# A two-part attention kernel: the last segment's memory answers move from the projection stage into the attention's row of turns, and the first turn's scores change banks

## The chip, the cores and the metric

The kernel runs on one core of a Trainium2 chip. The metric is the device time of one execution in microseconds (us); lower is better. A core has TensorE (matmuls; called PE in the profile), VectorE (DVE), ScalarE (ACT), GpSimd (POOL) and SyncE (SP, which here issues most DMA transfers).

## The reference

Two attentions are computed over 2048 tokens of width 576 with 32 heads of 18 columns, and set side by side. A is multi-query attention: all heads share one key and one value head. B splits the tokens into 4 segments of 512 and adds a memory of the earlier segments.

```python
# A
p = softmax(q_h @ k.T * Dh**-0.5);  o_h = p @ v;  out_A = concat(o_h) @ wo
# B, for segments s = 0..3, every head
p = softmax(causal(qs @ ks.T * scale));  a_dot = p @ vs
pq = phi(qs)                           # phi(t) = t + 1 if t > 0 else exp(t)
a_mem = (pq @ M) / (pq @ z + 1e-6)     # M, z from the segments before s
o = g * a_mem + (1 - g) * a_dot        # g = sigmoid(beta), one per head
M, z = M + phi(ks).T @ vs, z + phi(ks).sum(0)
out_B = concat(o) @ wo
```

Asking the memory is thus two products for a segment: `pq @ M` (the numerator) and `pq @ z` (the denominator), for segments 1, 2 and 3.

## The kernel before

The first phase projects the queries, keys and values of A and then of B, segment by segment; a projection (`proj`, L261) is fourteen matmuls of split operands, in tiles of 126 rows (7 heads) and 512 tokens, five tiles for 32 heads. The queries are split into two parts and stored (`split2`, L125 on ScalarE and L127 on VectorE; `store_parts`), `phi` of them is made by ScalarE (L408, L414) and VectorE (L416, `qf`), and `magnitude` writes their absolute values (`aq`, L438), from which `bound` (L588) makes an upper bound of each head's scores in the tile `pu`; `shift_parts` turns it into the shift that is stored for the softmax (`sht`, L136). Where a segment is the last one, `ask` (L444) multiplies each tile's `qf` by the memory, ScalarE evicts it (L451) to `numB[3]`, and `total` (L592) makes the denominators, evicted to `denB[3]` (L627).

The second phase is the attention. Its TensorE, VectorE and ScalarE work is written in the order in which it is issued, as a row of 416 turns. A turn k has three scores (L945 for A, L953 for B; two matmuls each into one of three two-bank buffers called `E`), the exponentials of them (ScalarE, L963; the middle score of a turn is first copied to `W` by VectorE, L960, and then freed; some halves of a tile are done by VectorE as a polynomial, tiles `PD`, L919 to L926), one extra step of TensorE in the bank `F`, and the products with the values (L993, bank `O`) of the scores of turn k - 2. In turns 0 to 18 the extra step is a part of the value sums that the projection stage left over (L513, list `LATER`). From turn 20 (`ASK`) it is a step of the memory for segments 1 and 2 (`ask_memory`, matmuls at L852, two steps for each evicted tile, evictions by VectorE at L857 into `xh` and, for denominators, at L861 into `rb`), once in every turn whose scores are all A's. When memory is through, from turn 64, the extra step is a fill: eight matmuls of the output projection (L796). Blocks of B (one pair of turns) come between blocks of A (eleven turns for a block of four heads): turns 0 to 10 are A's, 11 to 18 B's, 19 to 29 A's, 30 to 37 B's, 38 to 48 A's, 49 to 52 B's, 53 to 63 A's.

All four segments' `qf` and the memories go through DRAM tensors (`qfB[s]`, `mzB`) to the attention, by transfers of SyncE's queue (`load_qf`; the load of `mzB` into the tile `woA` in `ask_memory`).

Of the kernel before, what the change touches and what calls it, by code (L numbers as in the profile page):

```python
# [22 lines left out]
C = 512  # L23
# [36 lines left out]
MZ = 126 + 32  # L60
WB = 1440

LATE_ASK, ASK = (1, 2), 20
LATER = [(2, 14), (3, 14), (0, 3), None, (0, 3), (0, 4), None, (0, 4), None, None, (1, 3), None, (1, 3), None, (1, 2), (1, 2), (1, 2), None, (1, 2)]
FLAG = (2, 9, 11)

# [12 lines left out]
def attention_pair_kernel(ctx, tc, a_xT, a_w, a_wo, b_xT, b_w, b_wo, b_beta, ident_d, hmask_d, bmask_d, cmask_d, sel_d, zmask_d, selx_d, sely_d, out):  # L79
# [82 lines left out]
    with ExitStack() as ph:  # L162
# [248 lines left out]
        def phi(src, R, nm, bufs, hold=lambda ins: ins, e=None):  # L411

            e = e or negative(src, R, hold)
            hold(nc.scalar.activation(e[:R], e[:R], AF.Exp, scale=-1.0))  # L414
            f = p2.tile([128, C], F32, name=nm, bufs=bufs)
            hold(nc.vector.scalar_tensor_tensor(f[:R], src, 0.0, e[:R], op0=ALU.max, op1=ALU.add))  # L416
            return f

        for s in range(NSEG):
# [17 lines left out]
                aqs[t] = p2.tile([128, C], BF, name="aq", bufs=5)  # L437
                hold(nc.scalar.activation(aqs[t][:R], pj[:R], AF.Abs))  # L438

            def ask(t, hold=lambda ins: ins):  # L440
                R = RT[t]
                pn = ps.tile([128, C], F32, name="mm", bufs=1)
                hold(
                    nc.tensor.matmul(  # L444
                        pn[:R], Mst[:R, t].rearrange("p h d -> p (h d)")[:, :R], fs[t][:R], start=True, stop=True
                    )
                )

                def answer():
                    nm = p2.tile([128, C], F32, name="nm", bufs=2)  # L450
                    hold(nc.scalar.activation(nm[:R], pn[:R], AF.Copy, scale=gt[:R, t : t + 1]))  # L451
                    nc.sync.dma_start(numB[s][126 * t : 126 * t + R], nm[:R])

                return answer


            for t in range(5):
                if s == t == 0:
                    pj = ahead
# [25 lines left out]
                if s == 0:  # L485
                    split_wpart(10 + t)
                    if t < 3:
                        load_wpart(12 + t)
            if s and not last:
                nc.sync.dma_start(qfB[s][: RT[4], 4], fs[4][: RT[4]])  # L490
            if s == 0:
                nc.vector.memset(gt, 0.0)
# [94 lines left out]
                R, rows = RT[t], slice(32 * (t % 4), 32 * (t % 4) + 32)  # L587
                hold(nc.tensor.matmul(pu[rows], kbB[:R, t], aqs[t][:R], start=t < 4, stop=t > 0))  # L588

            def total(pd, t):  # L590
                R, rows = RT[t], slice(32 * (t % 4), 32 * (t % 4) + 32)
                pin(nc.tensor.matmul(pd[rows], zst[:R, t], fs[t][:R], start=t < 4, stop=t > 0))  # L592

            for t in range(4) if last else []:
                pj = ps.tile([128, C], F32, name="pj", bufs=4)
                proj(pj[:126], wBh, wBl, xh, xl, 126 * t, 126, pin)
                answer = ask(t - 1 if t else 4, pin)
                if t < 2:
                    (fifth_bound if t else last_key)(pin)
                if t == 3:  # L600
                    pu, pd = (ps.tile([128, C], F32, name="nd", bufs=2) for _ in range(2))
                    for i in (0, 1, 2, 4):
                        total(pd, i)
                e = negative(pj[:126], 126, pin)
                magnitude(t, pj, pin)
                fs[t] = phi(pj[:126], 126, "qf", 5, pin, e)
                answer()
                if t == 3:
                    for i in range(5):
                        bound(pu, i, pin)  # L610
                    answer = ask(3, pin)
                    total(pd, 3)
                    pin(nc.vector.tensor_reduce(fm[:, 1 + s : 2 + s], pu, axis=AX.X, op=ALU.max))
                qp = split2(pt, pj[:126], 126, pin)
                store_parts(qp, 0, 126, qB[s], 7 * t, 7)
                if t == 3:
                    answer()
                    dn = p2.tile([128, C], F32, name="ph_e", bufs=2)
            if not last:
                pu = ps.tile([128, C], F32, name="nd", bufs=2)  # L620
                for t in range(5):
# [2 lines left out]
            sp = shift_parts(pt, pu, -BOUND_UP, C, 128)  # L624
            sent = nc.sync.dma_start(shB[s].rearrange("j r t -> r j t"), sp.bitcast(F32))
            if last:
                nc.vector.tensor_scalar(dn, pd, 1e-6, None, op0=ALU.add)  # L627
                nc.sync.dma_start(denB[s], dn)
# [383 lines left out]

    def by_dve(c, hg):

        return [x for n, x in enumerate(BY_DVE) if n < 2 or (c, hg) in third]

    def turn_of(c, hg):

# [47 lines left out]
    def finish(k, ab, c, hg):  # L1066
# [26 lines left out]

        def place():

            return (ab, c) in parts or len(parts) - filled[0] // FILL < 2 and asked[0] >= min(2, len(parts) + 1)

        def load(k, t):
            load_heads(ab, c, t)
# [31 lines left out]
    with tc.manual_schedule(engines={ENG.PE, ENG.Activation, ENG.DVE}):  # L1131
# [3 lines left out]
        for n, b in enumerate(blocks):  # L1135
            ms = [m for m in range(len(its)) if block_of[m] == n]
            items = [(m, k) for m in ms for k in range(2)]
            for out_, cut in ((turns, len(items) // 3), (prods, len(items) // 3 - 1)):
                ends_ = split(len(items), cut)
                out_ += [items[a:z] for a, z in zip(ends_, ends_[1:])]  # L1140
        at(ASK + 4, 0, lambda: True, lambda k: load_qf(2))

        def halve(hi, lo, src):
            nc.scalar.copy(hi, src)
# [63 lines left out]
        for k in range(len(turns) + 2):  # L1208
            now[0] = k
            exps = [scores(its[n], pr, i == 1) for i, (n, pr) in enumerate(turns[k])] if k < len(turns) else []  # L1210
            for i in (0, 2, 1) if len(exps) == 3 else range(len(exps)):
                exps[i]()
            if k in FLAG:
                loose_flag(k)
            if k < len(LATER) and LATER[k]:
                i, m = LATER[k]
                m0, pj = begun_value.pop(i) if i in begun_value else (0, psO.tile([128, C], F32, name="O" if i == 3 else "F"))
                if m0 + m < 14:
                    begun_value[i] = m0 + m, pj
                late_value(i, m0, m0 + m, pj, (pa.tile([128, D], F32, name="osb", bufs=2) if i > 1 else pa.tile([128, C], F32, name="oe", bufs=4))[:, :304] if m0 + m == 14 else None)  # L1220
            if k > len(turns):
                halve_heads(first, 0)
            if memory is None:
                whole = run_fill()
                while k >= len(turns) and not whole:
                    whole = run_fill()
                if filled[0] % FILL == 0 and k > len(turns):
                    fill.pop(0)
            elif k >= ASK and all(its[n][0] == "A" for n, pr in turns[k]) and next(memory, None) is None:
                memory = None  # L1230

            if k > len(turns):
# [346 lines left out]
```

## Time and profile before

| | |
|---|---|
| median of 3 runs (lowest, highest) | 1394.51 us (1393.42, 1395.25) |
| the profiled execution's own time | 1394.57 us |
| span of its instructions | 1392.9 us |
| busy in the span: TensorE, ScalarE, VectorE, GpSimd | 99%, 87%, 74%, 19% |

The profiled execution is one run, and the time outside its span is 1.7 us. The busy shares are means over stages that have different limits.

### The profile page before, as it was taken

The page shows a single profiled execution, that of the slowest core. Times are in us where ns is not written, and L with a number is a line of the kernel's source. Part 1 is how long each engine was busy: PE and PEld are TensorE (multiplying, and loading weights), DVE is VectorE, ACT ScalarE, POOL GpSimd, SP SyncE. Part 2 cuts the span into 40 slices and gives each one's busy share as a digit, 9 for nine tenths or more (in the row PEclk, how much of TensorE's full clock was granted, in tenths as well). Part 3 has the DMA queues.
Part 4 walks back from the last instruction along what each step waited for, and adds up shares of the span by engine and source line. Part 5 has one row for each costly group of instructions (what it writes and reads, how often), then busy time and mean ns, then how long its engine had stood idle before and what let it go on. Part 6 is the DMA issues. An engine that isn't in the chain of part 4 may idle for free.

```text
span 1392.9 us, 41210 instructions
## 1 busy us (share of the span) xinstructions
PE 1379.1 (99%) x17455; PEld 835.6 (60%) x17455; DVE 1032.6 (74%) x1509; ACT 1205.8 (87%) x1497; POOL 260.5 (19%) x388
## 2 busy tenths in 40 slices
PE   9999999999999999999999999999999999999998
PEld 6778888755554555555555555555555555555558
DVE  6565463388787887777888877876878778887884
ACT  4543453599999999999999999999999999999992
POOL 2462120012313211312110022113010220001002
PEclk9999999999999999999999999999999999999999
DMA  9876556575564545332322442232103321120023
GB/s 285 261 230 185 180 198 204 188 208 181 153 182 158 147 145 162 101 113 77 105 67 71 141 152 63 85 120 79 52 35 100 104 76 42 31 71 21 18 64 132
DMA packets 88638, 173.67 MB, mean 125 GB/s; under 512 B 12308, under 2 KB 20109, under 8 KB 88018
## 3 DMA queue, kind: packets, MB, share of 16 engines
q1 hardware_dynamic: 81614, 158.91, 36.6%
q0 software_dynamic: 2368, 7.13, 1.8%
q10 hardware_dynamic: 4464, 4.92, 1.1%
q8 instruction: 139, 2.28, 0.7%
q14 instruction: 53, 0.43, 0.1%
HBM read 99.65 MB, written 70.67 MB: 122 GB/s over the span
## 4 chain that ended last, share of the span: by engine, by line
PE 88%; DVE 4%; ACT 3%; DMA 2%; issue 1%; POOL 1%; SPq 0%; DVEq 0%; POOLq 0%; ACTq 0%
PE O L993 33%; PE E L945 20%; PE F L796 11%; PE pj L261 11%; PE E L953 3%; ACT P L963 3%; PE nd L513 2%; DVE W L960 2%; PE pj L513 2%; PE E L1280 2%; PE pj L293 1%; PE F L852 1%; PE F L513 1%; DMA wr<-b_w 1%; DMA vseg<-vB 0%
## 5 line engine op out<-in xcount | busy, mean ns | idle before, releaser
L963 ACT ACTIVATE P<-E 128x1024 f32<-128x1024 f32 (+1 forms) x800 | 783.4, 1066 | 2.0 <-PE E L945 1.6
L960 DVE COPY W<-E 128x1024 f32<-128x1024 f32 (+2 forms) x416 | 453.1, 1089 | 142.2 <-PE E L945 84.1
L993 PE MATMUL O<-P,VA 128*32 128x256 f32 x7504 | 506.8, 379 | 0.0
L963 ACT ACTIVATE P<-W 128x1024 f32<-128x1024 f32 (+1 forms) x330 | 366.8, 1112 | 6.8 <-DVE W L960 6.3
L993 PEld LDWEIGHTS O<-P,VA 128*32 128x32 f32 x7504 | 258.8, 110 | 137.7 <-issue 4.7
L945 PE MATMUL E<-xl,kstA 56*128 56x512 f32 x1920 | 317.3, 430 | 2.1 <-ACT P L963 1.8
L945 PEld LDWEIGHTS E<-xl,kstA 56*128 56x128 f32 x1920 | 155.0, 184 | 159.1 <-issue 94.7
L968 POOL TENSOR_SCALAR_AFFINE_SELECT P<-P 128x256 f32<-128x256 f32 (+1 forms) x192 | 94.6, 493 | 393.4 <-ACT P L963 384.1
L780 POOL TENSOR_TENSOR xh<-xh,rb 126x512 f32<-126x512 f32 (+1 forms) x55 | 70.7, 1308 | 428.7 <-DVE PD L926 185.1
L796 PE MATMUL F<-woB,xh 126*32 126x192 f32 (+1 forms) x1920 | 126.6, 338 | 0.0
L993 PE MATMUL O<-PD,VA 128*32 128x256 f32 x688 | 88.9, 379 | 0.0
L796 PEld LDWEIGHTS F<-woB,xh 126*32 126x32 f32 (+1 forms) x1920 | 38.6, 108 | 74.8 <-issue 69.6
L993 PE MATMUL O<-P,vseg 128*32 128x256 f32 (+2 forms) x1536 | 81.4, 344 | 0.3
L127 DVE TENSOR_TENSOR qp<-pj,qp 126x512 fp32r<-126x512 f32 (+1 forms) x54 | 36.9, 686 | 54.4 <-ACT ph_e L408 32.8
L1002 DVE COPY oe<-O 128x512 f32<-128x512 f32 x64 | 44.2, 691 | 42.6 <-PE O L993 40.8
L261 PE MATMUL pj<-xh,wBh 128*126 128x512 f32 x180 | 72.5, 403 | 0.0
L919 DVE TENSOR_SCALAR PD<-E 128x512 uint32<-128x512 f32 x86 | 59.2, 688 | 16.5 <-PE E L945 14.9
L261 PE MATMUL pj<-xh,wBl 128*126 128x512 f32 x180 | 71.0, 394 | 0.0
L125 ACT CAST qp<-pj 126x512 fp32r<-126x512 f32 (+1 forms) x54 | 31.5, 584 | 42.6 <-PE pj L261 32.6
L993 PEld LDWEIGHTS O<-P,vseg 128*32 128x32 f32 x1536 | 49.1, 110 | 25.3 <-issue 1.8
L796 PE MATMUL F<-woA,xh 126*32 126x192 f32 (+1 forms) x960 | 63.9, 338 | 0.0
L924 DVE SCALAR_TENSOR_TENSOR PD<-PD,n 128x512 f32<-128x512 f32 x86 | 59.5, 692 | 3.0
(238 smaller groups left out, 1570.1 us busy)
## 6 DMA issues: line engine op xcount, KB each, us to landing
stB<-kB SPq DMA_DIRECT2D x96, 144.0 KB
stB<-qB SPq DMA_DIRECT2D x32, 288.0 KB
xl<-qA SPq DMA_DIRECT2D x30, 288.0 KB
oA<-oe SPq DMA_DIRECT2D x32, 256.0 KB
oB<-oe SPq DMA_DIRECT2D x32, 256.0 KB
qA<-qp SPq DMA_DIRECT2D x16, 504.0 KB
kB<-qp SPq DMA_DIRECT2D x16, 504.0 KB
qB<-qp SPq DMA_DIRECT2D x16, 504.0 KB
```

The source lines that it names most:

```text
L261: hold(nc.tensor.matmul(dst, w[:, c0 : c0 + M], x, start=i == 0, stop=i == len(ops) - 1))
L513: nc.tensor.matmul(pj[:, :n], x, w, start=m == 0, stop=m == len(ops) - 1)
L780: ins = tc.keep_in_program_order(nc.gpsimd.tensor_tensor(dst, a, b, op=op))
L796: nc.tensor.matmul(dst[32 * j : 32 * j + 32], parts[ab, c][: RT[t], t, r0 : r0 + 32], wo[ab][: RT[t], t, c0 : c0 + n], start=start, stop=stop,
L919: v.tensor_scalar(y, e, EXP_A, EXP_B, op0=ALU.mult, op1=ALU.add)
L924: lambda: stt(p, p, POLY[1], u, op0=ALU.add, op1=ALU.mult),
L945: nc.tensor.matmul(e[:, j], kstA[rows, 128 * kt : 128 * kt + 128], st[rows, h, :], start=True, stop=True)
L960: gate.append(nc.vector.tensor_copy(src[:, hs, :n], e[:, hs, :n]))
L963: nc.scalar.activation(p[:, hs, :n], src[:, hs, :n], AF.Exp, scale=SCALE)
L968: nc.gpsimd.affine_select(diag, diag, pattern=[[0, 2], [0, m], [1, 128]], base=0, channel_multiplier=-1, compare_op=ALU.is_ge, fill=0.0)
L993: nc.tensor.matmul(o[32 * j : 32 * j + 32, q0 : q0 + n], v, p[:, j % 2, p0 : p0 + n], start=m == hf == 0, stop=last and hf == 1,)
L1002: nc.vector.tensor_copy(osb, o)
```

## The change

`LATE_ASK` now holds segment 3 too. So the last segment's `ask` and `total` in the projection stage, the eviction of its answers and of its denominators go; its `qf` is stored to `qfB[3]` as the other segments' are, and the memory after segment 2 goes to `mzB`, which is loaded whole (2370 columns in place of 1580). In the attention there are 36 memory steps in place of 24, and they stand in every turn from 20 to 55, those with B's scores (30 to 37, 49 to 52) included. Segment 3's `qf` is asked for at turn 32 or later, once segment 1 has been asked. In the last segment's tiles the split of the queries stands ahead of `phi`. In turn 0 a dummy buffer of `E` is taken, so that its scores take the other two banks first; its value sums (14 matmuls) stand between its second score and its third, no score of turn 0 is copied by VectorE, and VectorE no longer does a half tile of block (0, 0).

```diff
-LATE_ASK, ASK = (1, 2), 20
+LATE_ASK, ASK = (1, 2, 3), 20
...
-            if s and not last:
+            if s:
                 nc.sync.dma_start(qfB[s][: RT[4], 4], fs[4][: RT[4]])
...
-                answer = ask(t - 1 if t else 4, pin)
                 if t < 2:
                     (fifth_bound if t else last_key)(pin)
-                if t == 3:
-                    pu, pd = (ps.tile([128, C], F32, name="nd", bufs=2) for _ in range(2))
-                    for i in (0, 1, 2, 4):
-                        total(pd, i)
                 e = negative(pj[:126], 126, pin)
                 magnitude(t, pj, pin)
-                fs[t] = phi(pj[:126], 126, "qf", 5, pin, e)
-                answer()
+                qp = split2(pt, pj[:126], 126, pin)
+                store_parts(qp, 0, 126, qB[s], 7 * t, 7)
+                f = phi(pj[:126], 126, "qf", 5, pin, e)
+                nc.sync.dma_start(qfB[s][:126, t], f[:126])
                 if t == 3:
+                    _, pu = (ps.tile([128, C], F32, name="nd", bufs=2) for _ in range(2))
                     for i in range(5):
                         bound(pu, i, pin)
-                    answer = ask(3, pin)
-                    total(pd, 3)
                     pin(nc.vector.tensor_reduce(fm[:, 1 + s : 2 + s], pu, axis=AX.X, op=ALU.max))
-                qp = split2(pt, pj[:126], 126, pin)
-                store_parts(qp, 0, 126, qB[s], 7 * t, 7)
-                if t == 3:
-                    answer()
...
-        return [x for n, x in enumerate(BY_DVE) if n < 2 or (c, hg) in third]
+        return [x for n, x in enumerate(BY_DVE) if (n or c or hg) and (n < 2 or (c, hg) in third)]
...
-            return (ab, c) in parts or len(parts) - filled[0] // FILL < 2 and asked[0] >= min(2, len(parts) + 1)
+            return (ab, c) in parts or len(parts) - filled[0] // FILL < 2 and asked[0] >= min(3, len(parts) + 2)
...
+        at(ASK + 12, 0, lambda: asked[0] >= 1, lambda k: load_qf(3))
...
+            if k == 0:
+                psE.tile([128, 2, 512], F32, name="E")
+            exps = []
+            for i, (n, pr) in enumerate(turns[k]) if k < len(turns) else []:
+                if k == 0 and i == 2:
+                    late_values(k)
+                exps.append(scores(its[n], pr, i == 1 and k > 0))
+            for i in (0, 2, 1) if len(exps) == 3 and k else range(len(exps)):
+                exps[i]()
...
-            elif k >= ASK and all(its[n][0] == "A" for n, pr in turns[k]) and next(memory, None) is None:
+            elif k >= ASK and next(memory, None) is None:
                 memory = None
```

TensorE's row at the end of the last segment's projections and in turn 0, before (`kbB` and `aq` belong to the bounds, `mz` is the memory, `woB` holds the weights of the value sums there):

```order
L588 LDWEIGHTS kbB
L588 MATMUL nd<-aq,kbB 32x512
L444 MATMUL mm<-qf,mz 126x512
L592 MATMUL nd<-qf,mz 32x512
L945 MATMUL E<-st_126,kstA 128x512 x6
L513 MATMUL F<-woB,xh 128x288
```

and after (the line numbers are those of the changed kernel):

```order
L571 MATMUL nd<-aq,kbB 32x512
L914 MATMUL E<-st_127,kstA 128x512 x4
L496 MATMUL F<-woB,xh 128x288
L496 MATMUL F<-woB,xl 128x288
L496 MATMUL F<-woB,xh 128x288 x2
L496 MATMUL F<-woB,xl 128x288
L496 MATMUL F<-woB,xh 128x288 x2
L496 MATMUL F<-woB,xl 128x288
L496 MATMUL F<-woB,xh 128x288 x2
L496 MATMUL F<-woB,xl 128x288
L496 MATMUL F<-woB,xh 128x288 x3
L914 MATMUL E<-st_127,kstA 128x512 x8
```

The ask and the total between the last bound and the first score are gone; the first two scores (4 matmuls) follow the bounds at once, and the value sums in `F` stand ahead of the third score, whose two matmuls are followed by turn 1's six.

TensorE's row in turns 30 and 31, the first pair of B turns from turn 20 on, before:

```order
L953 MATMUL E<-stB 128x512 x4
L953 MATMUL E<-stB 128x384 x2
L993 MATMUL O<-P,VA 32x256 x8
L953 MATMUL E<-stB 128x384 x2
L953 MATMUL E<-stB 128x256 x2
L953 MATMUL E<-stB 128x128 x2
L953 MATMUL E<-stB 128x256 x2
L953 MATMUL E<-stB 128x128 x2
L993 MATMUL O<-P,VA 32x256 x6
```

and after:

```order
L922 MATMUL E<-stB 128x512 x4
L922 MATMUL E<-stB 128x384 x2
L821 MATMUL F<-xh,woA 32x256 x2
L821 MATMUL F<-xh,woA 8x256
L821 MATMUL F<-xh,woA 32x256
L962 MATMUL O<-P,VA 32x256 x8
L922 MATMUL E<-stB 128x384 x2
L922 MATMUL E<-stB 128x256 x2
L922 MATMUL E<-stB 128x128 x2
L922 MATMUL E<-stB 128x256 x2
L922 MATMUL E<-stB 128x128 x2
L821 MATMUL F<-xh,woA 32x256 x2
```

Between the scores and the products of each of these turns now stands a memory step.

VectorE's row around turn 43, after (the row of before has a single `xh` eviction there and no `rb`):

```order
L826 TENSOR_SCALAR xh<-F,gt 72x512
L830 TENSOR_SCALAR rb<-F 32x512
L892 SCALAR_TENSOR_TENSOR PD<-n 128x512
L893 SCALAR_TENSOR_TENSOR PD<-PD,n 128x512
L888 TENSOR_SCALAR PD<-E 128x512
L929 COPY W<-E 128x512
```

The pair of evictions `xh` and `rb`, which stood in turn 39 before, stands in turns 31 and 43 now; another is in turn 55 in both kernels.

## Rows read from the trace of the kernel before

**Rows 1.** The page, part 4: the chain that ended last, by engine.

```profile
PE 88%; DVE 4%; ACT 3%; DMA 2%; issue 1%; POOL 1%; SPq 0%; DVEq 0%; POOLq 0%; ACTq 0%
```

**Rows 2.** The chain of waits in time: start, us, what.

```profile
267.61 0.86 PE mm L444 x2
268.47 3.25 PE pj L261 x14
```

**Rows 3.** Timeline of TensorE, last segment to turn 4: start, us, engine, line, op.

```profile
261.93 0.40 PE L261 MATMUL pj<-xh,wBl 128*126 128x512 f32 x1
262.78 1.09 PE L444 MATMUL mm<-qf,mz 126*126 126x512 f32 x2 [0.45 <-DVE qf L416]
263.71 0.23 PE L556 MATMUL tr<-kmB,selx 126*72 126x1 f32 x2
...
271.55 1.02 PE L444 MATMUL mm<-qf,mz 126*126 126x512 f32 x2
...
276.80 0.96 PE L945 MATMUL E<-st,kstA 56*128 56x512 f32 x6
...
280.68 0.40 PE L513 MATMUL O<-woB,xh 128*128 128x288 f32 x1
...
282.76 0.96 PE L945 MATMUL E<-st,kstA 56*128 56x512 f32 x6
...
288.02 1.24 PE L945 MATMUL E<-st,kstA 56*128 56x512 f32 x6
```

**Rows 4.** Timeline of ScalarE, same stretch and turn 48's copied exponential.

```profile
272.24 0.59 ACT L438 ACTIVATE aq<-pj 126x512 bf16<-126x512 f32 x1
...
277.37 1.94 ACT L963 ACTIVATE P<-E 128x1024 f32<-128x1024 f32 x2 [0.75 <-PE E L945]
...
404.69 1.06 ACT L963 ACTIVATE P<-W 128x1024 f32<-128x1024 f32 x1 [0.83 <-DVE W L960]
```

**Rows 5.** Timeline of VectorE, the end of the projection stage.

```profile
275.49 0.68 DVE L127 TENSOR_TENSOR qp<-pj,qp 126x512 fp32r<-126x512 f32 x1
276.09 0.68 DVE L136 TENSOR_SCALAR sht<-nd 128x512 f32<-128x512 f32 x1
```

**Rows 6.** Timeline of TensorE, turns 40 to 42 and a pair with fills.

```profile
378.99 0.96 PE L945 MATMUL E<-xl,kstA 56*128 56x512 f32 x6
...
382.21 0.96 PE L945 MATMUL E<-xl,kstA 56*128 56x512 f32 x6
383.09 0.64 PE L852 MATMUL F<-xh,woA 126*32 126x256 f32 x8
383.55 1.48 PE L993 MATMUL O<-P,VA 128*32 128x256 f32 x24
384.96 0.97 PE L945 MATMUL E<-xl,kstA 56*128 56x512 f32 x6
...
448.37 0.91 PE L953 MATMUL E<-stB 56*128 56x512 f32 x6
449.20 0.53 PE L796 MATMUL F<-woB,xh 126*32 126x192 f32 x8
449.55 1.37 PE L993 MATMUL O<-P,vseg 128*32 128x256 f32 x24
...
453.07 0.92 PE L953 MATMUL E<-stB 56*128 56x512 f32 x6
```

**Rows 7.** Stretches: length, each engine's busy time, granted clock, DMA share, GB/s.

```profile
355.59:373.73 18.14, 17.61 (x254) 10.27 (x250) 10.98 (x12) 18.14 (x24) 10.19 (x22) 1.00 0.50 154
387.72:404.11 16.39, 16.37 (x230) 8.25 (x226) 15.74 (x25) 15.49 (x17) 0.00 (x0) 1.00 0.54 172
404.11:421.84 17.73, 17.13 (x239) 9.43 (x236) 12.94 (x19) 17.15 (x21) 5.91 (x12) 1.00 0.56 166
...
1387.00:1388.00 1.00, 0.64 (x5) 0.40 (x3) 0.27 (x1) 0.00 (x0) 0.00 (x0) 1.00 0.99 343
...
1389.00:1390.00 1.00, 0.00 (x0) 0.00 (x0) 0.00 (x0) 0.00 (x0) 0.00 (x0) 0.81 0.47 153
```

More of the change, by code (lines that the diff above doesn't have):

```diff
@@ L438, in magnitude @@
                 hold(nc.scalar.activation(aqs[t][:R], pj[:R], AF.Abs))
[L440 to L454, printed above, removed]
             for t in range(5):
@@ L588, in bound @@
                 hold(nc.tensor.matmul(pu[rows], kbB[:R, t], aqs[t][:R], start=t < 4, stop=t > 0))
-            def total(pd, t):
-                R, rows = RT[t], slice(32 * (t % 4), 32 * (t % 4) + 32)
-                pin(nc.tensor.matmul(pd[rows], zst[:R, t], fs[t][:R], start=t < 4, stop=t > 0))
             for t in range(4) if last else []:
@@ L596, in attention_pair_kernel @@
                 proj(pj[:126], wBh, wBl, xh, xl, 126 * t, 126, pin)
-                answer = ask(t - 1 if t else 4, pin)
                 if t < 2:
                     (fifth_bound if t else last_key)(pin)
-                if t == 3:
-                    pu, pd = (ps.tile([128, C], F32, name="nd", bufs=2) for _ in range(2))
-                    for i in (0, 1, 2, 4):
-                        total(pd, i)
                 e = negative(pj[:126], 126, pin)
                 magnitude(t, pj, pin)
-                fs[t] = phi(pj[:126], 126, "qf", 5, pin, e)
-                answer()
+                qp = split2(pt, pj[:126], 126, pin)
+                store_parts(qp, 0, 126, qB[s], 7 * t, 7)
+                f = phi(pj[:126], 126, "qf", 5, pin, e)
+                nc.sync.dma_start(qfB[s][:126, t], f[:126])
                 if t == 3:
+                    _, pu = (ps.tile([128, C], F32, name="nd", bufs=2) for _ in range(2))
                     for i in range(5):
                         bound(pu, i, pin)
-                    answer = ask(3, pin)
-                    total(pd, 3)
                     pin(nc.vector.tensor_reduce(fm[:, 1 + s : 2 + s], pu, axis=AX.X, op=ALU.max))
-                qp = split2(pt, pj[:126], 126, pin)
-                store_parts(qp, 0, 126, qB[s], 7 * t, 7)
-                if t == 3:
-                    answer()
-                    dn = p2.tile([128, C], F32, name="ph_e", bufs=2)
             if not last:
@@ L626, in attention_pair_kernel @@
             if last:
-                nc.vector.tensor_scalar(dn, pd, 1e-6, None, op0=ALU.add)
-                nc.sync.dma_start(denB[s], dn)
                 def late_value(i, m0, m1, pj, v, xh=xh, xl=xl, value_sums=value_sums):
@@ L1206, in halve_heads, with late_values @@
             mixed(x[:88, 1], hi[:88, 1], raws[key], some[:88, 1:2])
[L1208 to L1214, printed above, removed]
+        def late_values(k):
             if k < len(LATER) and LATER[k]:
@@ L1220, in attention_pair_kernel @@
                 late_value(i, m0, m0 + m, pj, (pa.tile([128, D], F32, name="osb", bufs=2) if i > 1 else pa.tile([128, C], F32, name="oe", bufs=4))[:, :304] if m0 + m == 14 else None)
+        for k in range(len(turns) + 2):
+            now[0] = k
+            if k == 0:
[7 more added lines that the diff above has]
+                exps[i]()
+            if k in FLAG:
+                loose_flag(k)
+            if k:
+                late_values(k)
             if k > len(turns):
```

## Prediction

> **What bounds the kernel now.** I read the chain of waits first. Its shares name the engine to which the time goes: TensorE 88%, VectorE 4%, ScalarE 3% [rows 1]. So a microsecond that TensorE is spared, or no longer waits, arrives at the end, unless the stretch where it falls is one in which another engine ends last. Next I read TensorE's timeline over the two places that the change touches, the end of the last segment [rows 3] and the turns from 20 on, where a memory step stands in the row of matmuls [rows 6]. Last came the busy time by stage [rows 7]: it says who is full in each stretch. From turn 30 to the start of turn 38 (355.59 to 373.73, eight B turns without memory) ScalarE is busy 18.14 of 18.14 us, TensorE 17.61. From turn 43 to 49 VectorE is busy 15.74 of 16.39, TensorE 16.37. From turn 49 to 56 ScalarE has 17.15 and TensorE 17.13 of 17.73. So the new steps fall into stretches with three different limits, and each is priced apart. The profiled execution took 1394.57 us, 0.06 above the median of the runs, so the sum on it may be set against the median as it stands. What this kernel's measurement can tell from no change is taken as 0.2%, 2.8 us.
>
> **Start: three asks between projections.** On the chain two of them, alike, stand at 0.86 each; the later one is shown [rows 2]. The third also waits: the last projection matmul before it starts at 261.93, and the next matmul could start 0.23 later (14 of them take 3.25 [rows 2]), at 262.16; the ask waits 0.45 for VectorE's `qf` and the next work starts at 263.71 [rows 3]: 1.55. Together 3.27. The last projection, over at 271.55 before, is over at 268.28.
>
> **Start: from the last projection to turn 2.** Before, asks, totals and bounds fill 271.55 to 276.80, where the first score starts [rows 3]. After, only the five bounds stand there. Three are ready; the fourth needs `aq`, which ScalarE begins 3.27 earlier, at 268.97, and ends 0.59 later [rows 4], at 269.56. With two bounds behind it the first score starts at about 270.0, 6.8 us earlier. Turn 0 now issues only two scores (three take 0.88 before the next step, 382.21 to 383.09 [rows 6]), until 270.6, and then the value sums in bank F, whose bank `pu` held. That needs VectorE: the new order there is the split's subtraction (after ScalarE's cast, which follows `aq` and is over at about 270.05), `qf`, the maximum `fm`, the shift `sht`. These start 0.60 apart and the last lasts 0.68 [rows 5], so `sht` ends at 272.53 and TensorE stands from 270.6 to about 272.6. Fourteen value sums take 2.08 (280.68 to 282.76, the same sums in the other bank [rows 3]): until 274.7. The third score follows, its exp starts 0.57 behind it (276.80 to 277.37) and lasts about 1.0 (two take 1.94) [rows 3, 4], until 276.3. Turn 1's third score waits for that buffer, then come 2.08 of value sums, and turn 2 starts at 278.72, where it started at 282.76: **4.04 gained**. Before, turn 4's scores still took 1.24 in place of 0.96 because ScalarE was behind [rows 3]; with VectorE's half tile of turn 0 gone that is not needed: 0.28 more, bounds 0 and 0.28, and I take the upper since the exp is no longer split. **Gain 4.3.** Of the gap itself nothing is hidden: if `sht` were a microsecond later, turn 2 would be too.
>
> **Where there is no more gain.** The row of TensorE instructions from turn 57 on is the same in both kernels, memory ends at turn 55 in both, fills start at turn 64 in both. So nothing later is freed or added; the sum is made of turns 0 to 56.
>
> **Turns 30 to 37, eight new steps.** A step costs TensorE 0.46 (383.09 to 383.55 [rows 6]). A pair of B turns with two fills of 0.35 (449.20 to 449.55) takes 4.70 where TensorE is full (448.37 to 453.07 [rows 6]), so 4.00 bare and 4.92 with two steps. Four pairs: 19.7 against 18.14 [rows 7], **+1.5**: of 3.7 us of steps, 2.1 hide behind ScalarE and the rest stands out, as TensorE becomes the bound. VectorE's evictions for them hide: it is busy 10.98 of 18.14 there [rows 7]. Bounds: 0.5 if TensorE's slack in the first turns is larger than I see, 3.7 if none hides.
>
> **Turn 40.** It takes 3.22 (378.99 to 382.21) where the next turn takes 2.75 (to 384.96) [rows 6], as TensorE there waits for a pair of evictions, `xh` and `rb`. That pair moves to turns 31 and 43: **-0.47**.
>
> **Turn 43.** The pair's second eviction is new here, a `rb` of about 0.68 by its nearest row (a start every 0.60, each 0.68 long [rows 5]; I take the longer). VectorE has 0.65 us free in the whole stretch [rows 7], and the stretch's last copy already makes ScalarE wait 0.83 at 404.69 [rows 4]. So I let all of it pass on: **+0.68**, bounds 0 and 0.68.
>
> **Turns 49 to 55, four new steps.** 1.8 us of matmuls, beside 0.60 us in which TensorE stood (17.73 less 17.13 [rows 7]) and ScalarE that is nearly full. Their two pairs are B turns like those of 30 to 37, where a pair goes from 18.14 / 4 = 4.54 to 4.92, so 0.38 each: **+0.8**, bounds 0 (all in TensorE's waits) and 1.8.
>
> **Loads.** Segment 3's `qf` now comes back from memory for turn 44, asked for at turn 34, ten turns or some 25 us ahead; the larger weight load lies ahead of turn 20. I cost them at nothing, with the idle queues as cover; each microsecond that the load is later than turn 44 would cost one.
>
> **Sum.** -4.3 + 1.5 - 0.47 + 0.68 + 0.8 = -1.8, which from the median gives **1392.7 us**.
>
> **Rivals.** *Covered steps (0.20).* ScalarE and VectorE take the steps in, so that turns 43 and 49 to 55 cost 0.0 to 0.3, as the first bounds allow. For it: TensorE stands 0.60 us in the latter stretch. Against it: VectorE's stretch is full. 4.3 less 1.0 gives 1391.2.
> *The clock (0.15; ends slower).* TensorE stands about 2.0 us from 270.6. At the end of the run the granted clock was 1.00 in the slice in which the last matmul ended, 0.64 into it, and 0.81 in the second slice behind it [rows 7]: it fell from the 2.4 to the 1.2 GHz level about 2.0 us after the last matmul. If it falls in this gap, 2.08 of value sums and a score double, +2.4, and the second 2.08 too if it stays, +4.5: 1395.1 to 1397.2. It decides against the change from 1.8 us lost. The doubling is an estimate: no matmul of this trace ran at the lower level. The Trainium skill, TensorE: Matmul & The Clock Gate, in Part 1 on the clock gate, says that the array's resting state is half its clock and that only sustained work releases it, so that idle gaps are to be kept out of a matmul kernel. By that rule this rival would hold and its 1395.1 or more would be the time, if this gap is enough for it; no run here shows a gap of this length with work on both sides.
> *Steps at full price (0.10).* If the stretches with B turns were limited by TensorE after all, twelve steps of 0.46 are 5.5: -4.3 + 5.5 - 0.47 + 0.68 = +1.4, 1395.9. Against it: ScalarE's 18.14 of 18.14.
> *A late load (0.05).* `qf` of segment 3 or the stores ahead of it in SyncE's queue hold up turn 44: 1 to 5 us, 1394 to 1398.
>
> **How the numbers follow.** The forecast holds 0.50 and lies between 1391.3 and 1394.0 by its terms' bounds. The range reaches down to the covered steps with a little more start, 1390.6, and up to the clock and the full price, 1396.2; it leaves out the dearest clock and load cases and the cheapest start, below 2 in 10. Faster by over 0.2% means under 1391.7: a fifth of the forecast and most of the covered case, with some room for a start that I priced too low, 0.30. Slower means over 1397.3: parts of the clock, the full price and the load, 0.09. The rest, 0.61, is no change.
>
> **What the profile after would show.** The first score near 270.0 and turn 2 near 278.7; TensorE's gap of about 2 us in turn 0 with the granted clock at 1.00 behind it (a clock below that is the second rival). Turns 30 to 38 over in about 19.7 us with TensorE full and ScalarE no more. Turn 40 near 2.75. VectorE full from 43 to 49 and ScalarE waiting more than 0.83 for the copy near the start of turn 49. From turn 57 on every turn shifted by the same 1.8. The prediction is wrong if `sht` or the value sums are held by something else, if the B turns take the steps for nothing or at full price, or if TensorE waits in turn 44 for the load.

## Result and profile after

The changed kernel takes 1398.84 us (median of 7 runs, 1396.21 to 1403.9), the kernel before 1394.51 (1393.34 to 1395.25): a ratio of 1.0032, 95% interval 1.0016 to 1.0048. It is slower, and above the stated range. Its profiled execution took 1397.75 us, with a span of 1396.1.

TensorE's timeline of the changed kernel, from the last bounds to turn 2 (columns as in [rows 3]):

```profile
270.02 0.39 PE L571 MATMUL nd<-aq,kbB 126*32 126x512 bf16 x2 [0.85 <-ACT aq L438]
270.44 1.05 PE L914 MATMUL E<-st,kstA 56*128 56x512 f32 x4
273.11 0.58 PE L496 MATMUL F<-woB,xh 128*128 128x288 f32 x1 [1.61 <-DVE sht L136]
...
276.74 1.65 PE L914 MATMUL E<-st,kstA 56*128 56x512 f32 x6
...
281.17 0.96 PE L914 MATMUL E<-st,kstA 56*128 56x512 f32 x6
```

The first score starts at 270.44 (270.0 forecast), the value sums in `F` at 273.11 (272.6 forecast). But fourteen value sums take 3.63 (273.11 to 276.74) in place of 2.08 [rows 3], and turn 2 starts at 281.17, 1.59 earlier than before, not 4.04. The windows of single microseconds (columns as in [rows 7], the granted clock third from the end) say why:

```profile
271.00:272.00 1.00, 0.49 (x3) 0.06 (x1) 1.00 (x3) 0.71 (x1) 0.00 (x0) 0.84 0.53 199
272.00:273.00 1.00, 0.00 (x0) 0.00 (x0) 0.97 (x3) 1.00 (x2) 0.00 (x0) 0.50 0.83 240
...
277.00:278.00 1.00, 1.00 (x6) 0.56 (x6) 0.30 (x1) 0.43 (x1) 0.00 (x0) 0.50 0.65 137
278.00:279.00 1.00, 0.73 (x4) 0.19 (x2) 0.57 (x1) 1.00 (x2) 0.00 (x0) 0.75 0.65 240
279.00:280.00 1.00, 1.00 (x8) 0.92 (x7) 0.65 (x1) 1.00 (x2) 0.40 (x5) 1.00 0.81 152
```

The clock fell to the 1.2 GHz level in the gap and came back only in the slice from 278 to 279. The second loss is in turns 45 and 46. Again TensorE's timeline:

```profile
395.36 0.74 PE L914 MATMUL E<-xl,kstA 56*128 56x512 f32 x4
...
398.35 0.80 PE L914 MATMUL E<-xl,kstA 56*128 56x512 f32 x2 [2.25 <-DVE W L929]
399.08 1.08 PE L821 MATMUL F<-xh,woA 126*32 126x256 f32 x8
...
402.05 0.97 PE L914 MATMUL E<-xl,kstA 56*128 56x512 f32 x6
```

Turn 46 takes 6.69 us where an A turn with a step takes 2.75 [rows 6]. TensorE waits 2.25 for VectorE's copy. In VectorE's timeline, and in the chain of waits (start, us, what), one sees what that copy stands behind:

```profile
396.67 0.55 DVE L714 RECIPROCAL sm<-sm 112x64 f32<-112x64 f32 x1 [2.34 <-DMA sm<-oB]
```

```profile
382.87 5.75 DMA xl<-qA
388.64 8.00 DMA sm<-oB
396.67 0.04 DVE sm L714
396.70 0.43 issue
397.14 1.17 DVE W L929
398.31 0.04 issue
398.35 0.80 PE E L914 x2
```

`sm<-oB` reads back from DRAM the softmax sums of B's first segment, for VectorE to invert. Its transfer is issued at 388.64 and is there 8.00 us later; VectorE, which works in a fixed order, stands for it, the copy `W` stands behind it, TensorE behind the copy, and the clock falls a second time:

```profile
397.00:398.00 1.00, 0.00 (x0) 0.00 (x0) 1.00 (x2) 0.00 (x0) 0.00 (x0) 0.98 0.87 246
398.00:399.00 1.00, 0.65 (x2) 0.29 (x2) 1.00 (x3) 0.67 (x1) 0.00 (x0) 0.50 0.86 215
...
402.00:403.00 1.00, 1.00 (x14) 0.54 (x14) 0.88 (x3) 0.92 (x2) 0.00 (x0) 1.00 1.00 342
```

The stages, each from a turn's first score to the next stage's, answer to [rows 7]:

```profile
353.73:373.45 19.72, 19.72 (x318) 11.90 (x314) 14.21 (x17) 19.39 (x25) 10.78 (x23) 1.00 0.52 164
386.80:407.34 20.54, 18.25 (x230) 8.88 (x226) 17.33 (x26) 15.62 (x18) 0.00 (x0) 0.92 0.81 249
407.34:425.22 17.88, 17.88 (x270) 10.16 (x266) 13.69 (x19) 17.59 (x22) 5.94 (x12) 1.00 0.52 160
```

Turns 30 to 37 have TensorE full (19.72 of 19.72). Turns 43 to 48 take 20.54 where they took 16.39. Set against the kernel before, the changed one is 1.86 us ahead at turn 30 (353.73 against 355.59), 0.28 ahead at turn 38, 0.92 ahead at turn 43, 3.23 behind at turn 49 and 3.38 behind at turn 56; the spans differ by 3.2. What the forecast missed lies in turns 0 and 43 to 48.

### The profile page after: what moved, and what is told of

Read it like the earlier page. It is cut to its first block, busy times and chain, and to the rows that moved or that the text cites. A ratio compares the mean times of both kernels' runs of the same rounds, so it can differ in the third digit from the quotient of the medians.

```text
span 1396.1 us, 41363 instructions
## 1 busy us (share of the span) xinstructions
PE 1380.1 (99%) x17531; PEld 838.2 (60%) x17531; DVE 1032.7 (74%) x1507; ACT 1204.5 (86%) x1492; POOL 260.9 (19%) x389
## 4 chain that ended last, share of the span: by engine, by line
PE 75%; DVE 3%; ACT 2%; DMA 1%; issue 1%; SPq 0%; DVEq 0%; ACTq 0%
PE O L962 34%; PE E L914 20%; PE F L765 11%; PE E L922 4%; PE E L1261 2%; ACT P L932 2%; DVE W L929 1%; PE F L821 1%; PE pj L261 1%; PE F L496 1%; DMA sm<-oB 1%; DMA xl<-qA 0%; DVE sm L714 0%; PE nd L496 0%; DVE PD L892 0%
## 5 line engine op out<-in xcount | busy, mean ns | idle before, releaser
L932 ACT ACTIVATE PD<-W 128x512 f32<-128x512 f32 x85 | 60.3, 709 | 1.6 <-DVE W L929 1.6
```

The costliest lines, as they stand in the source:

```text
L932: nc.scalar.activation(p[:, hs, :n], src[:, hs, :n], AF.Exp, scale=SCALE)
```

## Experiments

Two theories stood against each other. One: there are two separate losses, the fallen clock in turn 0 and the wait for the read-back, and the steps cost what the forecast said. The other: the stretches are short of TensorE or VectorE, and the waits only show where. Each run below is against the changed kernel, whose median is 1398.84; the ratios are to the kernel before, run again beside each of them. Positions are those of one profiled execution each, and they drift: the last projection matmul, with the same work ahead of it, starts between 267.14 and 269.99 in the changed kernel and its variants. So lengths in turn 0 are also counted from the last two bounds (270.02 in the changed kernel).

**Filling the gap of turn 0 (warm).**

```diff
-                psE.tile([128, 2, 512], F32, name="E")
+                spare = psE.tile([128, 2, 512], F32, name="E")
...
                 if k == 0 and i == 2:
+                    for j in range(8):
+                        rows = slice(HALF[j % 2], HALF[j % 2] + KR)
+                        nc.tensor.matmul(spare[:, j % 2], kstA[rows, 0:128], st0[rows, 0, :], start=True, stop=True)
                     late_values(k)
```

> Changed kernel with eight more score matmuls (into the spare two-bank buffer that turn 0 takes, results unused) put into TensorE's gap of turn 0, between the second score and the value sums. Theory (the gap lets the granted clock fall, and the fall is the loss): the granted clock stays at 1.00 from 271 to 279, the fourteen value sums take 2.1 us instead of 3.6, turn 2 starts near 278.9 in place of 281.17, and the run is 2.0 to 2.6 us shorter than the changed kernel's, so 1395.5 against the 1397.75 of its profiled run, if the wait in turn 46 stays as it is. Rival (the sums are slow because their loads or banks are late, not the clock): the sums take 3.6 us as before and nothing is gained; or the eight matmuls come on top and cost up to 1.7 us.

Measured: median 1396.22 (1393.9 to 1401.0), ratio to the kernel before 1.0012, interval 0.9999 to 1.0025. TensorE's timeline of this run:

```profile
269.79 0.39 PE L571 MATMUL nd<-aq,kbB 126*32 126x512 bf16 x2 [0.85 <-ACT aq L438]
...
271.60 1.19 PE L1196 MATMUL E<-st,kstA 56*128 56x512 f32 x8 [0.31 <-DVE qf L416]
272.88 0.37 PE L496 MATMUL F<-woB,xh 128*128 128x288 f32 x1
...
274.90 0.96 PE L914 MATMUL E<-st,kstA 56*128 56x512 f32 x6
...
279.03 0.96 PE L914 MATMUL E<-st,kstA 56*128 56x512 f32 x6
...
351.57 0.73 PE L922 MATMUL E<-stB 56*128 56x512 f32 x4
...
398.63 0.56 PE L914 MATMUL E<-xl,kstA 56*128 56x512 f32 x2 [4.71 <-DVE W L929]
```

```profile
272.00:273.00 1.00, 0.91 (x9) 0.46 (x6) 0.96 (x3) 1.00 (x2) 0.00 (x0) 1.00 0.95 299
```

The sums start 3.09 behind the last two bounds, as in the changed kernel, and take 2.02 (272.88 to 274.90); the granted clock is 1.00 in each slice; turn 2 starts at 279.03, turn 30 at 351.57. From the last two bounds to turn 2 it is 9.24 in place of 11.15, so the fall cost 1.9 there. Against the kernel before, the start with the clock held gains 355.59 - 351.57 = 4.02. In this execution the wait in turn 46 has grown from 2.25 to 4.71: VectorE's inversion comes at 396.95 (396.67 in the changed kernel), so being early is paid back there, and the execution's own time, 1398.12, gained nothing. Over all runs it is not so: the median is 2.6 lower than the changed kernel's, though the two intervals overlap.

**The shift ahead of the split and `phi` (shift_first).** The bounds, the maximum and the shift of the last tile are written ahead of `split2` and `phi`.

```diff
-    def shift_parts(pool, u, neg_scale, n, R):
+    def shift_parts(pool, u, neg_scale, n, R, hold=lambda ins: ins):
...
-        nc.vector.tensor_scalar(t[:R, :n], u, neg_scale, None, op0=ALU.mult)
+        hold(nc.vector.tensor_scalar(t[:R, :n], u, neg_scale, None, op0=ALU.mult))
...
                 magnitude(t, pj, pin)
-                qp = split2(pt, pj[:126], 126, pin)
-                store_parts(qp, 0, 126, qB[s], 7 * t, 7)
-                f = phi(pj[:126], 126, "qf", 5, pin, e)
-                nc.sync.dma_start(qfB[s][:126, t], f[:126])
                 if t == 3:
...
                     pin(nc.vector.tensor_reduce(fm[:, 1 + s : 2 + s], pu, axis=AX.X, op=ALU.max))
+                    sp = shift_parts(pt, pu, -BOUND_UP, C, 128, pin)
+                qp = split2(pt, pj[:126], 126, pin)
+                store_parts(qp, 0, 126, qB[s], 7 * t, 7)
+                f = phi(pj[:126], 126, "qf", 5, pin, e)
+                nc.sync.dma_start(qfB[s][:126, t], f[:126])
...
```

> Changed kernel in which VectorE makes the maximum and the shift of the last segment before the split's subtraction and phi of the last tile, so that the bank of the value sums is free two VectorE operations earlier. Theory (TensorE's gap in turn 0 is VectorE's queue ahead of the shift, and the clock falls because of its length): the value sums start 1.2 us earlier, near 271.9, directly behind the second score or with a gap under 0.6 us, the granted clock stays at 1.00 and turn 2 starts near 277.6, 3.5 us earlier than in the changed kernel; the run is 2.5 to 3.5 us shorter than the changed kernel's. Rival (the two scores ahead of the sums need banks that the split and phi still read): the first scores or turn 1's scores wait instead, and turn 2 starts no more than 0.5 us earlier.

Measured: median 1395.84 (1394.74 to 1400.15), ratio to before 1.0013, interval 1.0003 to 1.0023: 3.0 us off the median. TensorE's and VectorE's timelines:

```profile
271.78 0.37 PE L496 MATMUL F<-woB,xh 128*128 128x288 f32 x1 [0.40 <-DVE sht L136]
...
278.17 0.96 PE L916 MATMUL E<-st,kstA 56*128 56x512 f32 x6
```

```profile
394.60 0.55 DVE L716 RECIPROCAL sm<-sm 112x64 f32<-112x64 f32 x1 [3.24 <-DMA sm<-oB]
```

The value sums start at 271.78 after a wait of 0.40, the clock stays at 1.00, turn 2 starts at 278.17 (277.6 expected; turn 0's third score and turn 1's waited a little). The wait for the copy in turn 46 has grown to 3.17, but the inversion comes at 394.60, 2.1 sooner than in the changed kernel: here the read-back moves with the start, and most of the 2.97 gained at turn 30 (350.76) comes through.

**The inversion three turns later (late_inv).**

```diff
-        d0, d1, d2, d3 = (0, 2 if hg == 6 else 5, 0, 3) if last else (2, 5, 3, 5) if (ab, c) == ("B", 0) else (2, 4 if ab == "B" and hg == 6 else 5, 3, 6)
+        d0, d1, d2, d3 = (0, 2 if hg == 6 else 5, 0, 3) if last else (2, 8, 3, 5) if (ab, c) == ("B", 0) else (2, 4 if ab == "B" and hg == 6 else 5, 3, 6)
```

> Changed kernel in which VectorE inverts the sums of B's first segment three turns later (48 and on in place of 45). Theory (VectorE stood 2.34 us in turn 45 for the transfer that reads these sums back, TensorE stood 2.25 us behind it in turn 46, and the clock fell after that): VectorE's wait there is gone, TensorE has no gap above 0.5 us from turn 43 to 49, the granted clock stays at 1.00 there, and the run is about 3 to 4 us shorter than the changed kernel's median: 1394 to 1395.5. It also scatters less than the 7.7 us between the changed kernel's lowest and highest run. Rival (the stretch is VectorE-bound by the moved evictions, the transfer only being where the wait shows): the wait moves to another instruction and the run is within 1 us of the changed kernel's.

Measured: median 1394.53 (1392.49 to 1397.42), ratio to before 1.0004, interval 0.9994 to 1.0015; the range of the runs shrank from 7.7 to 4.9. No wait of TensorE above 0.2 us is left from turn 43 to 56, and the stages read:

```profile
386.74:403.36 16.62, 16.58 (x231) 8.36 (x227) 15.87 (x23) 15.31 (x17) 0.00 (x0) 1.00 0.91 271
403.36:421.58 18.22, 18.00 (x270) 10.24 (x266) 14.90 (x23) 17.52 (x21) 5.91 (x12) 1.00 0.50 158
```

16.62 in place of 20.54. This one wait, with the clock's fall behind it, is worth 4.3 us of the median (3.9 by the ratios), as much as the whole loss.

**Turn 0 as it was (old_turn0).** The spare buffer, the value sums ahead of the third score and the dropped half tile are undone.

```diff
-        return [x for n, x in enumerate(BY_DVE) if (n or c or hg) and (n < 2 or (c, hg) in third)]
+        return [x for n, x in enumerate(BY_DVE) if n < 2 or (c, hg) in third]
...
-            if k == 0:
-                psE.tile([128, 2, 512], F32, name="E")
...
-                if k == 0 and i == 2:
-                    late_values(k)
-                exps.append(scores(its[n], pr, i == 1 and k > 0))
+                exps.append(scores(its[n], pr, i == 1))
...
```

> Changed kernel with turn 0 as it was: three scores, one of them copied, then the value sums, the usual banks, VectorE's half tile of block (0, 0) back. Theory (the gap of turn 0 is the shift's lateness, and the two scores ahead of the sums leave too little work to cover it): the third score covers 0.3 us more of the gap, so TensorE stands 1.2 to 1.4 us ahead of the sums in place of 1.6; the clock may then stay. With it at 1.00 turn 2 would start near 278.6, with a fall near 281. Rival (the first bank is held by phi and the split): the first score starts only when these are through, 1.2 us later, and turn 2 starts at 279 to 280 although the clock stays at 1.00.

Measured: median 1399.04 (1396.21 to 1401.86), no different from the changed kernel. The third score now waits 0.30 for `qf` and the sums 0.79 for the shift; the clock falls all the same, but is back by 276 (TensorE's timeline, then slices of the windows):

```profile
270.94 0.50 PE L914 MATMUL E<-st,kstA 56*128 56x512 f32 x2 [0.30 <-DVE qf L416]
272.23 0.47 PE L496 MATMUL F<-woB,xh 128*128 128x288 f32 x1 [0.79 <-DVE sht L136]
```

```profile
272.00:273.00 1.00, 0.77 (x4) 0.80 (x5) 0.93 (x3) 0.51 (x1) 0.00 (x0) 0.67 0.84 264
...
275.00:276.00 1.00, 1.00 (x6) 0.72 (x6) 0.14 (x1) 0.13 (x1) 0.00 (x0) 0.62 0.91 311
276.00:277.00 1.00, 1.00 (x8) 0.59 (x7) 1.00 (x4) 0.71 (x1) 0.00 (x0) 1.00 0.70 217
```

Turn 2 starts at 278.70, 2.5 earlier than in the changed kernel, but 0.9 of that lies ahead of turn 0 (the last two bounds start at 269.14). VectorE waits 2.58 for `sm<-oB`, little more than the changed kernel's 2.34, and this execution, the fastest of the ten, is 1.5 faster than the changed kernel's; why the median shows none of it is not known. The expectation that a fall of the clock would put turn 2 near 281 was wrong: the low stretch was shorter. That need not be the edit's doing, as the last section shows.

**Old turn 0 with the late inversion (old_late).** Both edits above.

> Changed kernel with turn 0 as it was in the kernel before, and the late inverses. With the old turn 0 alone turn 2 started at 278.70 in place of 281.17, but the time did not fall. Theory (the read-back, which lands at a fixed time, took that gain back): with the late inverses it comes through, turn 30 near 351.6, and the median is 1.5 to 2.5 us below the run with late inverses alone (1394.53), so 1392.0 to 1393.0: the part of the change in turn 0 loses time. Rival (the old turn 0 pays its start back in VectorE's backlog): turn 30 is no earlier than 353 and the median is within 0.7 us of 1394.53.

Measured: median 1395.27 (1391.46 to 1400.77), ratio to before 1.0004, interval 0.9988 to 1.002. The median was expected at 1392.0 to 1393.0, so the expectation failed. Turn 30 starts at 352.21 (351.6 expected), 1.5 earlier than in the changed kernel, and the fastest runs are at 1391.5 to 1393; but the runs scatter by 9 us, and in the profiled one TensorE waits 1.42 at 453.27, among the first turns with fills, for another load (`stB<-ones_d`). Whether turn 0's part of the change gains or loses stays open. By the start alone it loses: from the last two bounds to turn 30 it is 82.41 in both runs with the old turn 0, and 83.32 in the two executions with the new one (qf_at40, no_load) in which the clock was low about as long. The median doesn't show it.

**Another queue for the load (qf_pool).**

```diff
+        queue = nc.gpsimd if s == 3 else nc.sync
-        nc.sync.dma_start(qfs[s][:126, :4], qfB[s][:126, :4])
+        queue.dma_start(qfs[s][:126, :4], qfB[s][:126, :4])
...
```

> Changed kernel in which segment 3's qf is loaded through GpSimd's queue in place of SyncE's. Theory (the read-back of the sums is late because it stands in SyncE's queue behind this load): the read-back is issued some 4 to 6 us earlier than 388.64, VectorE's wait of 2.34 us is gone or below 0.5 us, and the median is 3 to 4 us below the changed kernel's 1398.84. Rival (the transfers' own time is the limit, 1.1 MB more in the same stretch, whatever the queue): the read-back is issued earlier but lands at 395 to 397 as before, and the median stays at 1398 to 1399.

Measured: median 1401.04 (1398.76 to 1404.07), ratio to before 1.0047, interval 1.0034 to 1.006: no gain (the interval overlaps the changed kernel's). Both expectations failed: SyncE issues the read-back at 389.86, later than 388.64, since the store `oB<-oe` that it reads back has itself not landed (SyncE waits 5.1 us for it), and VectorE waits 4.88 for the read-back. Its place behind the load in SyncE's queue is not the whole cause.

**The load at turn 40 (qf_at40).**

```diff
-        at(ASK + 12, 0, lambda: asked[0] >= 1, lambda k: load_qf(3))
+        at(ASK + 20, 0, lambda: asked[0] >= 1, lambda k: load_qf(3))
```

> Changed kernel in which segment 3's qf is asked for at turn 40 in place of 34, so that it stands in SyncE's queue behind the first part of the read-back of the sums. Theory (queue order makes the read-back late): the read-back lands before turn 45 and VectorE's wait for it is gone; instead the load has only about four turns, 11 us, and TensorE may wait for it at turn 44, 0 to 4 us, so the median is 1394.5 to 1398. Rival (transfer time is the limit): VectorE's wait stays above 2 us and nothing is gained.

Measured: median 1400.82 (1398.13 to 1404.52), ratio to before 1.0049, interval 1.0034 to 1.0063. The timelines of SyncE's queue and of TensorE:

```profile
382.53 0.89 SPq L700 DMA_DIRECT2D sm<-oB  x1
383.47 0.55 SPq L798 DMA_DIRECT2D xh<-qfB  x1
```

```profile
395.26 1.08 PE L821 MATMUL F<-xh,woA 126*32 126x256 f32 x8 [5.90 <-DMA xh<-qfB]
```

With the read-back ahead of it, VectorE's wait is gone; the load, issued from 383.47 on, is there 11.8 us later, and TensorE waits 5.90 for it in turn 44 (0 to 4 expected). Neither of the two places tried has both transfers in time.

**Without the load (no_load).** GpSimd fills the tile with ones, at turn 40, so segment 3's memory answers are left out of the result.

```diff
-        at(ASK + 12, 0, lambda: asked[0] >= 1, lambda k: load_qf(3))
+        def no_load(k):
+            qfs[3] = px.tile([128, 5, C], F32, name="xh")
+            nc.gpsimd.memset(qfs[3], 1.0)
+
+        at(ASK + 20, 0, lambda: asked[0] >= 1, no_load)
```

> Changed kernel in which segment 3's qf isn't loaded (1.15 MB less through the transfer engines); GpSimd fills the tile with ones, so segment 3's memory answers are left out of the result, while every step, eviction and store stays. The two tries with another queue and another place in the queue showed that the read-back is no earlier by the queue alone. Theory (the transfers' own time in turns 34 to 45 is what makes the read-back late, and these bytes are the excess): the read-back is issued before 385 in place of 388.64 and lands ahead of its use; VectorE's wait of 2.34 us and TensorE's of 2.25 us in turns 45 and 46 are gone, and the median is that of the run with late inverses, 1394.5, within 1 us. Rival (the earlier memory steps' own stores, or the faster start by itself, move the read-back's use ahead of it): the wait stays above 1 us and the median above 1396.5.

Measured: median 1394.87 (1393.42 to 1397.32), ratio to before 1.0006, interval 0.9997 to 1.0015. SyncE's queue in the kernel before (first line) and in this run (second):

```profile
381.96 0.89 SPq L731 DMA_DIRECT2D sm<-oB  x1
385.06 5.59 SPq L700 DMA_DIRECT2D sm<-oB  x2
```

The read-back is issued at 385.06 and VectorE's wait is gone, with all steps, evictions and stores in place. So the load is what makes the read-back late enough to be waited for. It is not the whole delay: counted from the start of turn 30, the read-back is issued after 26.4 us in the kernel before, 30.2 here and 34.9 in the changed kernel, and what makes the first 3.8 is not shown. One way in which the load acts stands among SyncE's waits in the changed kernel:

```profile
SPq L676 <- DMA xh<-qfB: 4.6, 1, 4.6
```

SyncE stands 4.6 us until the load has landed before it issues `stB<-kB`, a load of keys, and the read-back stands behind that in its row.

**Control: the late inversion in the kernel before (before_late).** The edit of late_inv.

> Control: the kernel before with the sums of B's first segment inverted three turns later, as in the run that gained. Theory (the read-back is in time in the kernel before, so the delay by itself gives nothing): within 0.5 us of the kernel before, which is 1394.2. Rival (those turns are short of VectorE whichever kernel, and the delay helps by itself): 1 us or more faster than the kernel before.

Measured: median 1394.29 (1393.01 to 1398.25), ratio 1.0003, interval 0.9995 to 1.0012: no change. The delay gives only what the load took.

**Both repairs (shift_late): the version to keep.** The edits of shift_first and late_inv.

> Changed kernel with both edits that gained: VectorE's shift ahead of the split and phi of the last tile, and B's first segment's sums inverted three turns later. Theory (two separate losses, the fallen clock of turn 0 and VectorE's wait for the read-back, the first hidden by the second since the read-back lands at a fixed time): the gains add, turn 2 near 278.2, no gap over 0.5 us from turn 43 to 49, median 2.5 to 3.0 us below that of the kernel with the late inverses alone (1394.53), so 1391.5 to 1392.0, which is faster than the kernel before by about 2.2 us. Rival (the earlier start runs into another transfer that lands at a fixed time): the gain is eaten by a new wait after turn 30 and the median stays above 1393.5.

Measured: median 1391.76 (1390.1 to 1393.81), ratio to the kernel before 0.9979, interval 0.997 to 0.9988: 2.7 us faster than before, by the medians 7.1 faster than the change as it stood. Turn 2 starts at 278.61 (278.2 expected; the bounds are 0.4 later than in shift_first), and no wait of TensorE above 0.2 us is left from turn 43 to 49. The gains add: 3.0 and 4.3 each by itself, 7.1 together. So over the runs neither loss hid the other; that part of the theory is not borne out.

**The clock alone (warm_late).** The edits of warm and late_inv.

> Changed kernel with the eight spare matmuls that fill the gap of turn 0 and the late inverses. Here the value sums start no earlier than in the changed kernel, so against the run with late inverses alone (1394.53) only the clock differs. Theory (the fallen clock alone costs 281.12 - 279.03 = 2.1 us): median 1392.0 to 1393.0, 2.1 us below the run with late inverses and 0.6 to 0.9 us above the run that also moves the shift ahead (1391.76). Rival (the gain of that run came from the earlier sums, not the clock): within 0.8 us of 1394.53.

Measured: median 1393.27 (1391.14 to 1395.45), ratio to before 0.9993, interval 0.9984 to 1.0001. The value sums start 3.09 behind the last two bounds, as in the changed kernel, and turn 2 starts at 279.07 as in warm. The median is 1.3 below late_inv's where 1.5 to 2.5 was expected; by the ratios to before, 1.0004 and 0.9993, it is 1.5; from the profiled executions (1393.90 and 1392.03) it is 1.9, as much as lies between their turn 0s (11.12 and 9.24 from the last two bounds to turn 2). So most or all of what the fall costs there comes through. It is also 1.5 above shift_late, where 0.6 to 0.9 was expected: the earlier sums are worth something beside the clock.

## Why the prediction was wrong

It forecast 1392.7 and got 1398.84. Its terms, in its order:

- *Start, 4.3.* The gap in turn 0 was foreseen (2.0 forecast, 1.61 measured) and so was its price if the clock fell, but that rival was given 0.15. It was what happened: 1.86 gained at turn 30. With the clock held (warm) the same start gains 4.02. The mechanism and the size of the gain were right, the choice between the cases wrong: the clock was taken to stay at 1.00, judged by the end of the run, where it fell 2.0 us behind the last matmul, and here it fell 0.2 us behind the last score. The fall cost 1.9 up to turn 2, near the lower price named, 2.4.
- *Turns 30 to 37, +1.5.* 19.72 less 18.14 is +1.58. TensorE full, as said.
- *Turn 40, -0.47.* It takes 378.52 to 381.27, 2.75 in place of 3.22.
- *Turn 43, +0.68.* Without the wait for the read-back (late_inv) the stretch of turns 43 to 48 costs +0.23: 16.62 less 16.39. Most of the extra eviction is taken in.
- *Turns 49 to 55, +0.8.* +0.15 in the changed kernel, +0.49 in late_inv.
- *Loads, nothing.* **This is the step that failed.** "I cost them at nothing, with the idle queues as cover": the load was priced against its own use in turn 44, for which it was in time. What it delays is another transfer of the same stretch, the read-back of the sums for turn 45; the forecast didn't look at which other transfers were due then. Turns 43 to 48 take 4.15 more than before, and 3.9 of that is this wait with the clock's fall behind it. The rival of the late load named the right transfer, the wrong waiter, and a chance of 0.05. The load is also wholly new in this stretch: in the kernel before only segments 1 and 2 send their `qf` through DRAM, not all four, and segment 3's is 1152 KB.

The profiled execution came out 3.2 slower in place of 1.8 faster. Of these 5.0 us, 3.5 is turns 43 to 48 (4.15 in place of 0.68) and 2.4 the start; turns 49 to 55 gave 0.65 back.

With both losses taken out the terms as measured give -4.02 + 1.58 - 0.64 + 0.23 + 0.49 = -2.4 (0.64 is what turns 38 to 42 gain in all), and warm_late, the kernel that has just these, took 1392.03 in its profiled execution, 2.5 below that of the kernel before. Its median is only 1.0 below by the ratio, 0.9993, so the close agreement is that of one execution.

Two things stay open. How the load through GpSimd's queue, which leaves SyncE's row free, still makes the store `oB<-oe` late is not shown: the DMA share from 364 to 394 was 0.84 with it, 0.76 in the changed kernel, 0.76 without the load and 0.80 before, so the engines aren't full on average and the mean doesn't tell the cases apart. And the part of turn 0 that changes banks was not settled by itself (old_late).

## What to carry to other kernels

A transfer that is added must be priced against everything that is due on the transfer engines in its stretch, not only against its own first use: list what reads back from DRAM there, when each is issued and when it is needed, and move the consumer if it stands in a fixed order in front of other work. Where a start is pulled forward, a later wait for a transfer can give the gain back: warm's profiled execution gained 2 us at turn 2 and lost it in turn 46. But look at the median too, which kept the gain. And order the small operations that free a bank ahead of those that only feed stores: one such reordering on VectorE was worth about 3 us here.

## What was not expected of the hardware

The clock fell after less than the gap at the end of the run [rows 7]. In the changed kernel it fell at about 271.7, some 0.2 us after the last score's matmuls (270.44 + 1.05), with a gap of 0.85 shortly before. In old_turn0 it fell at about 272.3, behind a row of gaps of 0.85, 0.30 and 0.79, none of them as long as 1 us. In warm, with 0.85 and 0.31, and in shift_first, with 0.85 and 0.40, it stayed at 1.00. So the longest single gap doesn't tell it: the same 0.85 stands in all four.

Nor do the gaps together. The runs late_inv, qf_pool, qf_at40 and no_load have the turn 0 of the changed kernel, with the same gaps of 0.85 and 1.6. The slices of qf_pool (the first two lines) and of qf_at40:

```profile
270.00:271.00 1.00, 0.19 (x1) 0.00 (x0) 1.00 (x3) 1.00 (x2) 0.00 (x0) 0.93 0.57 209
281.00:282.00 1.00, 1.00 (x8) 0.78 (x8) 0.43 (x1) 0.00 (x0) 0.00 (x0) 0.95 0.63 149
272.00:273.00 1.00, 0.65 (x4) 0.68 (x5) 0.93 (x3) 0.47 (x1) 0.00 (x0) 0.93 0.87 289
276.00:277.00 1.00, 0.85 (x6) 0.31 (x4) 0.23 (x2) 0.60 (x1) 0.00 (x0) 0.86 0.68 170
```

The clock fell in all five executions, but at different places: 0.2 us behind the last score's matmuls in the changed kernel, 0.7 in qf_pool, and 2.1 in qf_at40, where the value sums were already running. In turn 46, too, TensorE stood 2.25 us in the changed kernel and the clock fell; it stood 2.51 us in old_turn0 and the clock stayed at 1.00 in each slice. The Trainium skill, TensorE: Matmul & The Clock Gate, in Part 1, says that the clock follows how busy the array has been. The trace agrees only so far: the clock stayed at 1.00 in the four executions in which the gap of 1.6 was filled or shortened (warm, warm_late, shift_first, shift_late), but the same work and gaps gave falls 0.2 to 2.1 us behind the last score.

After the falls the clock was back at different distances: 6.8 us in turn 0 of the changed kernel (271.7 to 278.5), about 10 in that of qf_pool, about 3.4 in those of qf_at40 and old_turn0 and in turn 46 of the changed kernel. So a fall's price can't be read off one run: from the last two bounds to turn 2, the five executions with the same turn 0 take 10.73 to 12.76, and warm, without a fall, 9.24. The price lay between 1.5 and 3.5 us.
